# A tiled gated block with local attention on one core: its second row tile by feature halves, weights loaded in another order, orders anew

## The chip, the cores and the metric

The kernel runs on one core of a Trainium2 chip. The engines of a core work side by side and wait for one another by semaphores: TensorE (PE, matrix products; its weight loads are a row of their own, PEld), VectorE (DVE), ScalarE (ACT), GpSimd (POOL) and SyncE (SP), which here issues DMA transfers alone. ScalarE and GpSimd issue DMAs too. The metric is the device time of one execution in microseconds (us), as the median of several runs. The profile comes from one execution, which has a time of its own; the span is the part of it that the profile shows.

## The reference

All arrays are bfloat16. `x` has 2048 rows of 512 features.

```python
D, Df, H, Dh, W, dil = 512, 1792, 32, 16, 8, 2
xn = layernorm(x)                         # (x - mean) / sqrt(var + 1e-5), per row
q, k, v = split(xn @ wqkv)                # 32 heads of 16
# row s sees the rows s, s-2, ..., s-14 (those below 0 are masked)
logits[h, s, w] = sum_d q[h, s, d] * k[h, s - 2*w, d] * Dh ** -0.5
o[h, s] = sum_w softmax_w(logits)[h, s, w] * v[h, s - 2*w]
s = o @ wo
g = silu((gelu(xn @ w_gate) * (xn @ w_up)) @ w_down)
out = x + s * g
```

## The kernel before

*Tiles and stages.* The 2048 rows are 16 tiles of 128 (numbered 0 to 15) and 4 blocks of 512 (0 to 3); block 0 is tiles 0 to 3. The stages of a block are: layer norm; turning the normed rows, so that features lie on partitions (`xT`); q, k, v (`qkv_ps`); the scores of 8 keys per row (products on VectorE, `prod`; their sums over a head, block 0 by TensorE into `L_ps`, blocks 1 to 3 by 16 accumulating GpSimd DMAs each into `Ls`, the "gathers"); softmax; the products with v (`pv`) and their sums; a trip of the attention output through DRAM, which turns it; gate and up products (`g_ps`, `u_ps`), gelu, their product `hT`; the down product `y_ps`, silu; the output product `s_ps`, its gate, the sum with x and the store.

*What sets the order.* The program is not written in its order. Each step is an `Op` with an engine, an assumed duration, the steps that it needs (a leading `~` means only the start of the other), the buffers that it takes and frees, and a priority. `schedule` (L126) plays them through as a list scheduler: on each engine, of the steps that could start within 0.05 us of the earliest one, that with the lowest priority. The instructions are then written out in the order of those planned starts, and nothing reorders them afterwards: on each engine, and on each engine's DMA queue, they are issued in that order and each waits for its own semaphores. The assumed durations (`DMA_FIXED`, `DMA_RATE` and so on) thus decide orders and nothing else. A priority is a base per stage and block (`N`, `S`, `V`, `Q`, `F`, `Y`, `O` in `PARAMS`), plus an offset per step, plus a number of its own from the list `nudge` (one per step, 854 in all).

*The start.* Before the first data TensorE runs matmuls on zeros (`warm`, L254). `loads` (L1131) gives the order of the input transfers as one chain. Tile 0's x comes in two feature halves of 256, the first issued by SP, the second by ACT (L1135), tile 1's x whole by SP. Then the weights of q and of k, each in two halves of 256 KB by contraction chunks (L1146): both halves of q by ACT, both of k by SP; then x of tiles 2 and 3, the two halves of v's weights, x of block 1, and the ffn weights, all by SP.

*Block 0 by tiles.* Tile 0 is done by `first_tile` (statistics L463, root L466, reciprocal L471, norm L475, transposes L483, each by feature halves; the first half's copy into `xT0` by ACT, L490, the second's by VectorE, L492). Tiles 1 to 3 are done by `layernorm`: statistics of tile 1 in two halves of one loaded tile, one norm of 512 (L348), four transposes on TensorE (L365), one copy of 512 by ACT (L374) or, for the tiles in `vcopy` (tile 1), by VectorE (L372). `qkv_tiles` (L600) makes q, k and v of each tile, 16 matmuls of 128x128 each (L612). For q and k of tile 0 these are split in two steps of 8 (`mm_q0_t0a` and so on), the first of which needs only the first feature half of x and of the weights. TensorE's order at the start is: tile 0's transposes; q and the first half of k of tile 0; tile 1's four transposes; k's second half; q and k of tile 1; v of tile 0; v of tile 1; tile 2's work. The x of blocks 1 to 3 is turned by DMA (L440).

*Later names.* Products with the keys L705 and their halving sums L717, L721; gathers L798; the maximum over keys L810; products with v L868 and sums L875; stores and load of the turned output L1018 and L1027; gate and up products L925, gelu L941, evacuation of up L949, their product L963; down L985, silu L1001; output product L1046.

Of the kernel before, what the change touches and what calls it, by code (L numbers as in the profile page):

```python
# [44 lines left out]
DMA_FIXED = 2.3  # L45
DMA_CROWDED = 3.5
LOADED = 40.0
DMA_RATE = {"SP": 325e3, "POOL": 180e3}
# [11 lines left out]
    sums=(3,), warm=4, slack=2.82, N=[306.5, 111.8, 418.2, 728.4], psum=(0,), rpow=False,  # L60
    S=[237.0, -554.0, 60.7, -257.2], V=[-277.9, -35.1, 276.7, -102.3], Q=[43.7, -338.2, 71.3, 36.8],
    F=[34.7, 79.8, 266.5, 442.4], Y=[-106.0, 20.0, -72.7, -105.7], O=[19.3, -380.8, -324.0, 455.3], vnorm=(),
    vcopy=(1,), vsum=(0,), crowd=1.35,
    nudge=[
# [44 lines left out]
    ],  # L109
)  # L110


# [115 lines left out]
class Kernel:  # L228
# [53 lines left out]
    def layernorm(self, j):  # L282
        base = self.when("N", j)
        for tt in range(TPB):
# [12 lines left out]
            def half_stats(i):  # L297
                h = D // 2
                self.nc.vector.bn_stats(out=self.stats1[:, i, :], in_=self.x_sb[:, 1, i * h : (i + 1) * h])  # L299
# [76 lines left out]
            if t == 0:  # L376
                self.first_tile()
                continue
# [924 lines left out]
```

## Time and profile before

| | |
|---|---|
| median of 3 runs | 213.8 us (213.67, 213.80, 214.13) |
| the profiled execution's own time | 213.45 us |
| its span | 211.6 us, 3097 instructions |
| TensorE / VectorE / ScalarE / GpSimd busy | 98% / 88% / 74% / 31% of the span |
| granted TensorE clock | 1.0 |
| DMA | 32.17 MB in 32991 packets, mean 152 GB/s |

A page gives, for one execution, the busy time of each engine; the span in 40 slices; the DMA queues; the chain of work that ended last, followed back from the last instruction; the costliest groups of instructions, with the busy time, the mean duration of one in ns, and the idle time of the engine just before them with what ended most of it; and the DMA issues with the time from issue to landing. Views of the trace give the same by line, by wait, by stretch of time, and in order of time. An engine that is busy for 98% of the span can only be finished sooner by the other 2%, or by doing less.

### The profile page before, as it was taken

How to read it: one execution, taken by the hardware profiler on the slowest of the kernel's cores; microseconds unless marked ns; L12 is line 12 of the kernel's file. 1: busy time of each engine (PE TensorE's matmuls, PEld its weight loads, DVE VectorE, ACT ScalarE, POOL GpSimd, SP SyncE). 2: the span in 40 equal slices, each digit the busy share in tenths (PEclk: the TensorE clock that was granted, in tenths of full speed). 3: DMA queues.
4: the chain of work that ended last, by engine and by line, in shares of the span. 5: the costliest groups of instructions: out<-in, count | busy, mean ns of one | idle time of the engine just before them, and what ended most of it. 6: DMA issues, size and time to landing. Idle time of an engine off the chain costs nothing.

```text
span 211.6 us, 3097 instructions
## 1 busy us (share of the span) xinstructions
PE 206.6 (98%) x1123; PEld 101.4 (48%) x1123; DVE 187.3 (88%) x215; ACT 156.5 (74%) x262; POOL 65.7 (31%) x108
## 2 busy tenths in 40 slices
PE   7999999999999999999999999999999999999994
PEld 2996444445444444444445444444444444444442
DVE  4698998499999997999999999999999989998124
ACT  3688999999999998679634888967323689666352
POOL 5041310002137688040369422379630011001000
PEclk9999999999999999999999999999999999999999
DMA  6999997200938587680797947378996059505822
GB/s 191 364 382 373 318 288 184 58 0 22 176 100 159 102 159 147 142 206 7 112 159 126 167 137 169 74 114 161 153 180 150 0 124 222 153 0 112 217 72 99
DMA packets 32991, 32.17 MB, mean 152 GB/s; under 512 B 17088, under 2 KB 29520, under 8 KB 32976
## 3 DMA queue, kind: packets, MB, share of 16 engines
q0 software_dynamic: 5136, 14.41, 36.3%
q1 hardware_dynamic: 27008, 16.95, 29.2%
q10 hardware_dynamic: 832, 0.62, 0.9%
q8 instruction: 9, 0.15, 0.3%
q14 instruction: 6, 0.05, 0.1%
HBM read 14.12 MB, written 6.31 MB: 97 GB/s over the span
## 4 chain that ended last, share of the span: by engine, by line
PE 94%; DVE 2%; DMA 1%; ACT 1%; issue 0%; SPq 0%
PE g_ps L925 23%; PE u_ps L925 23%; PE y_ps L985 22%; PE qkv_ps L528 15%; PE s_ps L1046 6%; PE qkv_ps L612 5%; DMA x_sb<-in_A_x_dram 1%; DVE s L1101 1%; DVE s L1107 0%; ACT s L1061 0%; ACT xnT L374 0%; PE L_ps L742 0%; PE tr_ps L365 0%; DVE xnT L372 0%; DVE stats L299 0%
## 5 line engine op out<-in xcount | busy, mean ns | idle before, releaser
L925 PE MATMUL g_ps<-xnT,wg_sb 128*128 128x512 bf16 x224 | 54.2, 380 | 0.0
L925 PE MATMUL u_ps<-xnT,wu_sb 128*128 128x512 bf16 x224 | 53.6, 379 | 0.0
L985 PE MATMUL y_ps<-wd_sb,hT 128*128 128x512 bf16 (+2 forms) x238 | 51.8, 367 | 0.0
L798 POOL DMA_DIRECT2D Ls<-prod x48 | 36.9, 872 | 27.2 <-DMA Ls<-prod 12.4
L941 ACT ACTIVATE gl<-g_ps 128x512 bf16<-128x512 f32 x56 | 31.9, 598 | 16.0 <-PE g_ps L925 12.8
L705 DVE TENSOR_TENSOR prod<-q_sb,k_sb 128x2048 bf16<-128x2048 bf16 x32 | 37.8, 1219 | 2.2 <-ACT q_sb L543 1.7
L949 ACT ACTIVATE hT<-u_ps 128x512 bf16<-128x512 f32 x56 | 32.1, 601 | 7.9 <-PE u_ps L925 6.8
L868 DVE TENSOR_TENSOR pv<-attn,v_arr 128x4096 bf16<-128x4096 bf16 x16 | 36.2, 2284 | 0.1
L985 PEld LDWEIGHTS <-hT 128*128 128x128 bf16 x238 | 22.7, 98 | 25.9
L925 PEld LDWEIGHTS <-wu_sb 128*128 128x128 bf16 x224 | 21.9, 98 | 26.4
L925 PEld LDWEIGHTS <-wg_sb 128*128 128x128 bf16 x224 | 21.7, 98 | 26.1 <-issue 0.4
L963 DVE TENSOR_TENSOR hT<-hT,gl 128x1024 bf16<-128x1024 bf16 x28 | 18.6, 683 | 3.0 <-ACT gl L941 2.6
L570 POOL DMA_DIRECT2D vT_dram<-vst x12 | 8.9, 745 | 35.5 <-ACT vst L550 35.4
L717 DVE TENSOR_TENSOR prod<-prod 128x2048 bf16<-128x2048 bf16 x16 | 19.2, 1220 | 0.0
L1061 ACT ACTIVATE s<-s_ps 128x512 bf16<-128x512 f32 x15 | 8.8, 597 | 12.6 <-PE s_ps L1046 12.6
L677 POOL DMA_DIRECT2D v_arr<-vT_dram x16 | 10.8, 719 | 16.3 <-DMA vT_dram<-vst 16.3
L1046 PE MATMUL s_ps<-wo_sb,oT_sb 128*128 128x512 bf16 (+2 forms) x68 | 15.6, 367 | 0.0
L875 DVE TENSOR_TENSOR pv<-pv 128x2048 bf16<-128x2048 bf16 x12 | 14.5, 1220 | 0.1
L941 ACT ACT_TABLE_LOAD x10 | 12.8, 1283 | 0.7 <-PE g_ps L925 0.6
L1001 ACT ACTIVATE sil<-y_ps 128x512 bf16<-128x512 f32 (+2 forms) x17 | 9.3, 574 | 5.3 <-PE y_ps L985 5.2
L1074 POOL DMA_DIRECT2D s<-x_sb x3 | 2.8, 930 | 31.3 <-DVE tot L835 15.7
L528 PE MATMUL qkv_ps<-xnT,wq_sb 128*128 128x512 bf16 x48 | 12.0, 379 | 0.0
(94 smaller groups left out, 230.3 us busy)
## 6 DMA issues: line engine op xcount, KB each, us to landing
Ls<-prod POOLq DMA_DIRECT2D x48, 128.0 KB, 3.5
v_arr<-vT_dram POOLq DMA_DIRECT2D x16, 142.0 KB, 4.4
vT_dram<-vst POOLq DMA_DIRECT2D x16, 128.0 KB, 3.7
pv<-pv POOLq DMA_DIRECT2D x4, 512.0 KB, 4.9
oT_dram<-o_sb SPq DMA_DIRECT2D x16, 128.0 KB, 3.4
oT_sb<-oT_dram SPq DMA_DIRECT2D x4, 512.0 KB, 4.7
wg_sb<-in_B_w_gate_dram SPq DMA_DIRECT2D x2, 896.0 KB, 9.9
wu_sb<-in_B_w_up_dram SPq DMA_DIRECT2D x2, 896.0 KB, 12.3
```

The source lines that it names most:

```text
L528: self.nc.tensor.matmul(ps[:], lhsT=self.w_qkv(which, dk, c), rhs=self.t[f"xT{j}"][:, dk, :], start=(dk == 0), stop=(dk == NC - 1),)
L705: self.nc.vector.tensor_tensor(out=self.t[pair][:, c % 2].rearrange("p n w t -> p w n t"), in0=q.unsqueeze(1).to_broadcast([P, W, 2, P]), ...
L717: self.nc.vector.tensor_tensor(out=pr[:, 0], in0=pr[:, 0], in1=pr[:, 1], op=ALU.add)
L798: self.nc.gpsimd.dma_start(out=self.t[f"Ls{j}"][H * tq : H * (tq + 1)], in_=self.t[f"pr{j}_{tq // 2}_0"][s::NC, 0, tq % 2], **(dict(accum_ ...
L868: self.nc.vector.tensor_tensor(out=pv[:], in0=self.t[f"at{j}"][:, 2 * i : 2 * i + 2, :].unsqueeze(2).to_broadcast([P, 2, DH, P]), in1=win, ...
L875: self.nc.vector.tensor_tensor(out=pv[:, 0], in0=pv[:, 0], in1=pv[:, 1], op=ALU.add)
L925: nc.tensor.matmul(ps[:], lhsT=w[:, dk, fc * P : (fc + 1) * P], rhs=self.t[f"xT{j}"][:, dk, :], start=(dk == 0), stop=(dk == NC - 1),)
L941: self.nc.scalar.activation(out=self.t[f"gl{j}_{pair}"][:, fc % 2, :], in_=self.t[f"ps_g{j}_{fc}"][:], func=AF.Gelu_apprx_tanh,)
L949: self.nc.scalar.activation(out=self.t[f"h{j}"][:, fc, :], in_=self.t[f"ps_u{j}_{fc}"][:], func=AF.Copy)
L963: self.nc.vector.tensor_tensor(out=h, in0=h, in1=self.t[f"gl{j}_{pair}"][:], op=ALU.mult)
L985: nc.tensor.matmul(self.t["ps_" + key][:, 0 : n1 - n0], lhsT=self.t[f"h{j}"][:, fc, tt * P : (tt + 1) * P], rhs=self.wd_sb[:, fc, n0:n1], ...
L1046: self.nc.tensor.matmul(ps[:, 0 : n1 - n0], lhsT=self.t[f"oT{j}"][:, c, tt * P : (tt + 1) * P], rhs=self.wo_sb[:, c, n0:n1], start=(c == 0 ...
```

## The change

- Tile 1 goes through the same function as tile 0, now `early_tile(t)`: its x is loaded in two halves (the first by SP, the second by ACT), with two statistics, two norms of 256, two pairs of transposes into buffers of their own and two copies of 256, both by VectorE. Its q is split in two steps of 8 matmuls, as tile 0's.
- Weights of q, k, v: the first halves of q and k are issued by ACT, the second halves by SP; v comes as one transfer of 512 KB.
- Tile 2's copy of 512 goes from ACT to VectorE (`vcopy`).
- Tile 3's statistics are not put before tile 2's.
- Two branches of code that did not run (`power`, `minus`) are removed, and a memset for one of them on GpSimd.
- The planner's assumed DMA durations, the bases of the priorities and the whole list `nudge` (now 858 numbers) are replaced.

The built program has the same 1123 matmuls. Its order on TensorE at the start: q of tile 0, first half of k, tile 1's transposes, second half of k, first half of q of tile 1, k of tile 1, v of tile 0, second half of q of tile 1, tile 2's transposes, v of tiles 1 and 2, then tile 3. On ACT's queue: second halves of x of tiles 0 and 1, first halves of q's and k's weights (the instruction for k's also waits for the landing of tile 0's half, whose DMA slot it uses again). On SP's: first halves of x of tiles 0 and 1, second halves of q's and k's weights, x of tiles 2 and 3, v's weights, x of block 1 and on as before. Later many steps stand elsewhere in their engine's order; the order of the last ones is the old one.

```diff
-DMA_FIXED = 2.3
-DMA_CROWDED = 3.5
+DMA_FIXED = 2.0
+DMA_CROWDED = 3.8
+SHARED = 1.14
 LOADED = 40.0
-DMA_RATE = {"SP": 325e3, "POOL": 180e3}
+DMA_RATE = {"SP": 370e3, "POOL": 180e3}
...
 PARAMS = dict(
-    sums=(3,), warm=4, slack=2.82, N=[306.5, 111.8, 418.2, 728.4], psum=(0,), rpow=False,
-    S=[237.0, -554.0, 60.7, -257.2], V=[-277.9, -35.1, 276.7, -102.3], Q=[43.7, -338.2, 71.3, 36.8],
-    F=[34.7, 79.8, 266.5, 442.4], Y=[-106.0, 20.0, -72.7, -105.7], O=[19.3, -380.8, -324.0, 455.3], vnorm=(),
-    vcopy=(1,), vsum=(0,), crowd=1.35,
+    sums=(3,), psum=(0,), warm=4, slack=2.52, N=[340.7, 50.8, 416.1, 741.4], S=[213.7, -605.4, 61.2, -265.3],
+    V=[-291.2, -67.1, 282.9, -169.4], Q=[-35.5, -339.1, 71.0, 39.1], F=[17.7, 79.3, 268.5, 442.6],
+    Y=[-110.3, 20.9, -73.3, -165.5], O=[19.3, -378.8, -317.6, 380.6], vnorm=(), vcopy=(2,), vsum=(0,),
+    crowd=1.35,
     nudge=[
...
-            if t == 0:
-                self.first_tile()
+            if t < 2:
+                self.early_tile(t)
                 continue
...
-            elif t == 1:
-                self.op("stats1_0", "DVE", 0.34, ["ld_x1_0", "~aggr0"], lambda f=half_stats: f(0), prio=prio)
-                self.op("stats1_1", "DVE", 0.34, ["ld_x1_0", "~norm0_1"], lambda f=half_stats: f(1), prio=prio)
-                self.op("aggr1", "DVE", 0.16, ["stats1_0", "stats1_1"], half_aggr, prio=prio)
             else:
                 self.op(f"stats{t}", "DVE", 0.61,
-                        [f"ld_x{t if j == 0 else j}_{j}"] + (["copy1"] if t == 2 else []), stats, prio=prio,
+                        [f"ld_x{t if j == 0 else j}_{j}"] + {2: ["copy1"], 3: ["~aggr2"]}.get(t, []), stats, prio=prio,
...
-    def first_tile(self):
+    def early_tile(self, t):
 
         h = D // 2
         xn = {}
 
         def stats(i):
-            self.nc.vector.bn_stats(out=self.stats0[:, i, :], in_=self.x_sb[:, 0, i * h : (i + 1) * h])
+            self.nc.vector.bn_stats(out=self.stats2[:, t, i, :], in_=self.x_sb[:, t, i * h : (i + 1) * h])
 
         def aggr():
-            self.nc.vector.bn_aggr(out=self.mv[:, 0, :], in_=self.stats0[:])
+            self.nc.vector.bn_aggr(out=self.mv[:, t, :], in_=self.stats2[:, t])
 
         def root():
             self.nc.scalar.activation(
-                out=self.rstd[:, 0, :], in_=self.mv[:, 0, 1:2], func=AF.Sqrt, bias=self.eps[:]
+                out=self.rstd[:, t, :], in_=self.mv[:, t, 1:2], func=AF.Sqrt, bias=self.eps[:]
             )
 
         def inverse():
-            self.nc.vector.reciprocal(out=self.rstd[:, 0, :], in_=self.rstd[:, 0, :])
+            self.nc.vector.reciprocal(out=self.rstd[:, t, :], in_=self.rstd[:, t, :])
 
         def norm(i):
-            xn[i] = self.new(f"xn0_{i}", [P, h], BF16, "xn")
+            xn[i] = self.new(f"xn{t}_{i}", [P, h], BF16, "xn")
             self.nc.vector.tensor_scalar(
-                out=xn[i][:], in0=self.x_sb[:, 0, i * h : (i + 1) * h], scalar1=self.mv[:, 0, 0:1],
-                scalar2=self.rstd[:, 0, :], op0=ALU.subtract, op1=ALU.mult,
+                out=xn[i][:], in0=self.x_sb[:, t, i * h : (i + 1) * h], scalar1=self.mv[:, t, 0:1],
+                scalar2=self.rstd[:, t, :], op0=ALU.subtract, op1=ALU.mult,
             )
 
         def turn(i):
-            ps = self.new(f"tr0_{i}", [P, 2, P], BF16, "tr_ps")
+            ps = self.new(f"tr{t}_{i}", [P, 2, P], BF16, "tr_ps")
             for c in range(2):
                 self.nc.tensor.transpose(ps[:, c, :], xn[i][:, c * P : (c + 1) * P], self.ident[:])
 
         def copy(i):
-            if i == 0:
+            if t == i == 0:
                 self.new("xT0", [P, NC, TQ], BF16, "xnT")
-            out = self.t["xT0"][:, 2 * i : 2 * i + 2, 0:P]
-            if i == 0:
+            out = self.t["xT0"][:, 2 * i : 2 * i + 2, t * P : (t + 1) * P]
+            if t == i == 0:
                 self.nc.scalar.activation(out=out, in_=self.t["tr0_0"][:], func=AF.Copy)
             else:
-                self.nc.vector.tensor_copy(out=out, in_=self.t["tr0_1"][:])
-
-        prio = -60.0
+                self.nc.vector.tensor_copy(out=out, in_=self.t[f"tr{t}_{i}"][:])
+
+        prio = -60.0 + 10 * t
+        order = {(1, 0): ["~aggr0"], (1, 1): ["~norm0_1"]}
         for i in range(2):
-            self.op(f"stats0_{i}", "DVE", 0.34, [f"ld_x0_0{'ab'[i]}"], lambda i=i: stats(i), prio=prio)
-        self.op("aggr0", "DVE", 0.1, ["stats0_0", "stats0_1"], aggr, prio=prio)
-        self.op("root0", "ACT", 0.25, ["aggr0"], root, prio=prio, table="sqrt")
-        self.op("rstd0", "DVE", 0.07, ["root0"], inverse, prio=prio)
+            self.op(f"stats{t}_{i}", "DVE", 0.34, [f"ld_x{t}_0{'ab'[i]}"] + order.get((t, i), []), lambda i=i: stats(i),
+                    prio=prio)
+        self.op(f"aggr{t}", "DVE", 0.16, [f"stats{t}_0", f"stats{t}_1"], aggr, prio=prio)
+        self.op(f"root{t}", "ACT", 0.27, [f"aggr{t}"], root, prio=prio, table="sqrt")
+        self.op(f"rstd{t}", "DVE", 0.1, [f"root{t}"], inverse, prio=prio)
         for i in range(2):
-            self.op(f"norm0_{i}", "DVE", 0.26, ["rstd0"] + ["~norm0_0"] * i, lambda i=i: norm(i), take=[("xn", f"xn0_{i}")],
-                    use=[f"xn0_{i}"], prio=prio + i)
-            self.op(f"turn0_{i}", "PE", 2 * MM128, [f"norm0_{i}"] + ["~turn0_0"] * i, lambda i=i: turn(i),
-                    take=[("F", f"tr0_{i}")], use=[f"xn0_{i}", f"tr0_{i}"], prio=prio)
-        self.op("copy0_0", "ACT", 0.28, ["turn0_0"], lambda: copy(0), take=[("xT", "xT0")],
-                use=["tr0_0", "xT0"], prio=prio)
-        self.op("copy0", "DVE", 0.22, ["turn0_1", "~copy0_0"], lambda: copy(1), use=["tr0_1", "xT0"], prio=prio)
+            self.op(f"norm{t}_{i}", "DVE", 0.26, [f"rstd{t}"] + [f"~norm{t}_0"] * i, lambda i=i: norm(i),
+                    take=[("xn", f"xn{t}_{i}")], use=[f"xn{t}_{i}"], prio=prio + i)
+            self.op(f"turn{t}_{i}", "PE", 2 * MM128, [f"norm{t}_{i}"] + [f"~turn{t}_0"] * i, lambda i=i: turn(i),
+                    take=[("F", f"tr{t}_{i}")], use=[f"xn{t}_{i}", f"tr{t}_{i}"], prio=prio)
+            name = f"copy{t}" + "_0" * (1 - i)
+            need = [f"turn{t}_{i}"] + ([f"~copy{t}_0"] if i else ["copy0"] if t else [])
+            self.op(name, "DVE" if t or i else "ACT", 0.24 if t or i else 0.3, need, lambda i=i: copy(i),
+                    take=[] if t or i else [("xT", "xT0")], use=[f"tr{t}_{i}", "xT0"], prio=prio)
...
-                if t == 0 and which < 2:
+                if (t, which) in ((0, 0), (0, 1), (1, 0)):
                     half = NC * NC // 2 * MM128
-                    self.op(f"mm_{key}a", "PE", half, ["copy0_0", weights + "a"], lambda f=mms: f(0, 2), take=take,
+                    self.op(f"mm_{key}a", "PE", half, [f"copy{t}_0", weights + "a"], lambda f=mms: f(0, 2), take=take,
                             use=use, prio=prio)
-                    self.op(f"mm_{key}", "PE", half, [f"mm_{key}a", "copy0", weights], lambda f=mms: f(2, NC),
+                    self.op(f"mm_{key}", "PE", half, [f"mm_{key}a", f"copy{t}", weights], lambda f=mms: f(2, NC),
...
-        x0 = [("ld_x0_0a", lambda: x_tile(0, 0, D // 2), kb),
-              ("ld_x0_0b", lambda: x_tile(0, D // 2, D, "scalar"), kb),
-              xt[1]]
+        early = [(f"ld_x{t}_0{'ab'[i]}", lambda t=t, i=i: x_tile(t, i * D // 2, (i + 1) * D // 2, ("sync", "scalar")[i]),
+                  64 * kb if t or i else kb) for t in range(2) for i in range(2)]
         h = NC // 2
-        wq = [("ld_wqa", lambda: w_qkv(0, 0, h, "scalar"), 256 * kb), ("ld_wq", lambda: w_qkv(0, h, NC, "scalar"), 256 * kb)]
-        wk = [("ld_wka", lambda: w_qkv(1, 0, h), 256 * kb), ("ld_wk", lambda: w_qkv(1, h, NC), 256 * kb)]
-        wv = [("ld_wva", lambda: w_qkv(2, 0, h), 256 * kb), ("ld_wv", lambda: w_qkv(2, h, NC), 256 * kb)]
+        wq = [("ld_wqa", lambda: w_qkv(0, 0, h, "scalar"), 256 * kb), ("ld_wq", lambda: w_qkv(0, h, NC), 256 * kb)]
+        wk = [("ld_wka", lambda: w_qkv(1, 0, h, "scalar"), 256 * kb), ("ld_wk", lambda: w_qkv(1, h, NC), 256 * kb)]
+        wv = [("ld_wv", lambda: w_qkv(2), 512 * kb)]
         xb = [(f"ld_x{j}_{j}", lambda j=j: x_block(j), 512 * kb) for j in range(NJ)]
-        seq = x0 + wq + wk + [xt[2], xt[3]] + wv + [xb[1]]
+        seq = early + wq + wk + [xt[2], xt[3]] + wv + [xb[1]]
...
-                    nbytes=int(nbytes * (self.par["crowd"] if i >= len(seq) - 5 else 1)))
+                    nbytes=int(nbytes * (1.0 if i < 12 else SHARED if i < len(seq) - 5 else SHARED * self.par["crowd"])))
```

More of the change, by code (lines that the diff above doesn't have):

```diff
@@ L295, in aggr @@
                 nc.vector.bn_aggr(out=self.mv[:, t, :], in_=self.stats[:, t, :])
-            def half_stats(i):
-                h = D // 2
-                self.nc.vector.bn_stats(out=self.stats1[:, i, :], in_=self.x_sb[:, 1, i * h : (i + 1) * h])
-            def half_aggr():
-                self.nc.vector.bn_aggr(out=self.mv[:, 1, :], in_=self.stats1[:])
             def root(t=t):
@@ L330, in product @@
                 )
-            def power(a, b, k):
-                nc = self.nc
-                r = self.rstd[:, a:b, 0]
-                nc.gpsimd.tensor_scalar(
-                    out=r, in0=self.mv[:, a:b, 1], scalar1=k, scalar2=EPS, op0=ALU.mult, op1=ALU.add
-                )
-                nc.gpsimd.tensor_tensor(out=r, in0=r, in1=self.mhalf[:, 0 : b - a], op=ALU.pow)
-                nc.gpsimd.tensor_tensor(out=self.nmr[:, a:b, 0], in0=self.mv[:, a:b, 0], in1=r, op=ALU.mult)
-            def minus(a, b):
-                m = self.mv[:, a:b, 0]
-                self.nc.vector.tensor_scalar(out=m, in0=m, scalar1=-1.0, scalar2=None, op0=ALU.mult)
             def norm_dve(t=t):
@@ L412, in layernorm @@
                 a, b = j * TPB, (j + 1) * TPB
-                if tt == 0 and self.par["rpow"]:
-                    need = [f"aggr{i}" for i in range(a, b)]
-                    if not by_act:
-                        self.op(f"minus{j}_", "DVE", 0.1, need, lambda f=minus, a=a, b=b: f(a, b), prio=prio)
-                        need = [f"minus{j}_"]
-                    self.op(f"shift{j}_", "POOL", 2.0, need,
-                            lambda f=power, a=a, b=b, k=1.0 / D if by_act else 1.0: f(a, b, k), prio=prio, slack=0.5)
-                elif tt == 0:
+                if tt == 0:
                     self.op(f"root{j}_", "ACT", 0.25, [f"aggr{i}" for i in range(a, b)],
@@ L430, in layernorm @@
                 self.op(f"norm{t}", "ACT", 0.75, [ready], norm_act, take=[("xn", f"xn{t}")],
-                        use=[f"xn{t}"], prio=prio, slack=(3.0 if self.par["rpow"] else 0.5) if j else 0.0)
+                        use=[f"xn{t}"], prio=prio, slack=0.5 if j else 0.0)
             else:
@@ L807, in gathered @@
                 before = [nm]
+        hot = -10.0
         def peak():
@@ L818, in less @@
             )
-        hot = -10.0
         self.op(f"peak{j}", "DVE", 1.9, [f"gat{j}_{tq}_{NC - 1}" for tq in range(TPB)], peak, use=[f"Ls{j}"], prio=hot)
@@ L1228 @@
     k.stats = cpool.tile([P, NT, nc.vector.BN_STATS_DIM], F32, name="stats")
-    k.stats1 = cpool.tile([P, 2, nc.vector.BN_STATS_DIM], F32, name="stats1")
-    k.stats0 = cpool.tile([P, 2, nc.vector.BN_STATS_DIM], F32, name="stats0")
+    k.stats2 = cpool.tile([P, 2, 2, nc.vector.BN_STATS_DIM], F32, name="stats2")
     k.mv = cpool.tile([P, NT, nc.vector.BN_AGGR_DIM], F32, name="mv")
     k.rstd = cpool.tile([P, NT, 1], F32, name="rstd")
-    k.mhalf = cpool.tile([P, TPB], F32, name="mhalf")
     k.eps = cpool.tile([P, 1], F32, name="eps")
@@ L1241 @@
     k.rs = cpool.tile([P, 2, P], BF16, name="rs")
+    k.ind = cpool.tile([P, H], BF16, name="ind")
     k.ident = cpool.tile([P, P], BF16, name="ident")
-    k.ind = cpool.tile([P, H], BF16, name="ind")
     k.mask = cpool.tile([H, W, PAD], F32, name="mask")
@@ L1252 @@
     make_identity(nc, k.ident[:])
-    nc.gpsimd.memset(k.mhalf[:], -0.5)
     nc.gpsimd.memset(k.ind[:], 1.0)
```

88 rows, old and new, of the table nudge are left out of this document.

## The prediction

> **What bounds the kernel now.** I read the page first (busy shares, chain), then the waits of PE, the chain in order of time, the busy time by stretch, and last the timeline and the landings of the loads.
>
> ```profile
> span 211.6 us, 3097 instructions
> ...
> PE 206.6 (98%) x1123; PEld 101.4 (48%) x1123; DVE 187.3 (88%) x215; ACT 156.5 (74%) x262; POOL 65.7 (31%) x108
> ...
> PE 94%; DVE 2%; DMA 1%; ACT 1%; issue 0%; SPq 0%
> ```
>
> The chain is PE for 94% of the span. An engine share can hide waits, so the next view is what PE waited for, then its busy time by stretch (each row: length, then PE, PEld, DVE, ACT, POOL, with counts, clock, DMA).
>
> ```profile
> PE warm_ps L254 <- DVE eps L1251: 1.3, 1, 1.3
> PE tr_ps L483 <- DVE xn L475: 0.2, 1, 0.2
> PE qkv_ps L612 <- ACT xnT L490: 0.2, 1, 0.2
> ```
> ```profile
> 20.00:35.00 15.00, 15.00 (x70) 6.64 (x68) 14.83 (x22) 14.37 (x25) 3.34 (x5) 1.00 1.04 289
> 125.00:150.00 25.00, 25.00 (x118) 11.30 (x117) 24.72 (x25) 20.02 (x34) 15.02 (x22) 1.00 0.65 130
> 150.00:175.00 25.00, 25.00 (x117) 11.30 (x116) 24.11 (x23) 11.93 (x19) 3.94 (x5) 1.00 0.58 118
> ```
>
> From 20 us on PE has no gap, at granted clock 1.00. No reordering can gain there; it can only lose. What is left to win lies in the start, so that is read in order of time:
>
> ```profile
> 5.07 0.30 PE tr_ps L483 x2
> ...
> 5.39 0.39 ACT xnT L490
> 5.78 0.04 issue
> 5.82 1.50 PE qkv_ps L612 x24
> ...
> 7.58 0.43 DVE xnT L372
> ...
> 8.06 2.85 PE qkv_ps L612 x48
> ...
> 11.43 0.60 ACT xnT L374
> ...
> 12.07 1.05 PE qkv_ps L612 x16
> ```
>
> The chain leaves PE three times after its first transposes: for tile 0's copy (5.39), tile 1's copy (7.58) and tile 2's copy (11.43). The timeline prices the last two (a group's length includes the last matmul's tail, so starts are compared):
>
> ```profile
> 3.94 0.29 ACT L466 ACTIVATE rstd<-mv,eps 128x1 f32<-128x1 f32 x1 [0.70 <-DVE mv L463]
> 4.13 0.43 DVE L299 BATCH_NORM_STATS2 stats<-x_sb 128x6 f32<-128x256 bf16 x1 [0.23 <-DMA x_sb<-in_A_x_dram]
> 4.48 0.15 DVE L471 RECIPROCAL rstd<-rstd 128x1 f32<-128x1 f32 x1
> 7.16 0.39 PE L365 MATMUL tr_ps<-ident,xn 128*128 128x128 bf16 x4
> 7.38 0.61 PE L612 MATMUL qkv_ps<-xnT,wk_sb 128*128 128x128 bf16 x8
> 8.95 1.06 PE L612 MATMUL qkv_ps<-xnT,wk_sb 128*128 128x128 bf16 x16
> 9.84 1.05 PE L612 MATMUL qkv_ps<-xnT,wv_sb 128*128 128x128 bf16 x16
> 10.96 1.06 PE L612 MATMUL qkv_ps<-xnT,wv_sb 128*128 128x128 bf16 x16
> ```
>
> 16 of these matmuls take 9.84 − 8.95 = 0.89 us, one 0.0556; four transposes 7.38 − 7.16 = 0.22. The eight of k's second half end at 7.38 + 0.45 = 7.83, and q of tile 1 starts at 8.06: 0.23 us lost to tile 1's copy. The sixteen of v end at 10.96 + 0.89 = 11.85 and the next starts at 12.07: 0.22 lost to tile 2's copy.
>
> **The change part by part.**
>
> *x of tile 1 in halves on both queues.* VectorE stood 0.23 us for x1; its first statistics then ran into the time at which tile 0's reciprocal could have started (ACT's root was done at 3.94 + 0.29 = 4.23, the reciprocal came at 4.48). The halves go out right behind tile 0's, each ahead of all weights of its queue. If they land by 3.9, those statistics (0.43) start right before ACT's root and the reciprocal at about 4.28; everything of tile 0 moves up 0.20 and q's first matmul from 5.82 to 5.62. If they land as before, at 4.1, this is nothing. I take 0.20; the next term shows that it does not decide.
>
> *The weights' order.* Rows of q, k and v (issues, first and last start; landings after issue):
>
> ```profile
> L1146 ACTq DMA_DIRECT2D wq_sb<-in_A_wqkv_dram x2: 427/442/457, 1.2 to 1.8; - x2
> DMA to landing us min/median/max: 3.3/3.8/4.3
> ...
> L1146 SPq DMA_DIRECT2D wk_sb<-in_A_wqkv_dram x2: 435/452/469, 1.7 to 2.2; - x2
> DMA to landing us min/median/max: 4.2/4.4/4.6
> ...
> L1146 SPq DMA_DIRECT2D wv_sb<-in_A_wqkv_dram x2: 379/406/433, 3.7 to 4.5; - x2
> DMA to landing us min/median/max: 4.6/4.6/4.7
> ```
>
> So q's halves landed at 4.5 and 6.1, k's at 5.9 and 6.8, v's last at 9.1. Afterwards the first halves of q and k go out by ACT, the second halves by SP, so both halves of one matrix travel side by side. q's first half, issued at about 1.8 instead of 1.2 (ACT issues x1's half in its old place), should land between the old 4.5 and 6.1; I take the middle, 5.3, which is free, since it is needed at 5.62 (6.1 would cost 0.5). k's first half is the new risk: ACT's instruction for it also waits for tile 0's first x (a DMA slot that is used again), and it now shares the engines with k's second half. Bounds: 5.9, its old landing, and 6.8, where the second half, the last of the same 1,280 KB (x of two tiles, q, k), landed. I take 6.7, nearer to the later, because two equal halves end together. PE could start k at 5.62 + 16 × 0.0556 = 6.51; with 6.7 and the 0.04 that an issue costs it starts at 6.74, a new wait of 0.23, with tile 1's transposes behind it in PE's order.
>
> *Tile 1 by feature halves.* Behind k's first eight (to 7.19) and the transposes (to 7.41) stand k's second eight (to 7.85). VectorE's rows by shape:
>
> ```profile
> L348 DVE TENSOR_SCALAR xn<-x_sb,mv,rstd 128x512 bf16<-128x512 bf16 x2 | 0.8, 416 | 0.1
> L475 DVE TENSOR_SCALAR xn<-x_sb,mv,rstd 128x256 bf16<-128x256 bf16 x2 | 0.6, 343 | 0.0
> L372 DVE COPY xnT<-tr_ps 128x512 bf16<-128x512 bf16 x1 | 0.4, 424 | 0.8 <-PE tr_ps L365 0.8
> L492 DVE COPY xnT<-tr_ps 128x256 bf16<-128x256 bf16 x1 | 0.2, 237 | 0.0
> ```
>
> The first half's copy waits for two transposes (tail of 0.22 included, to about 7.5) and takes 0.24 in place of 0.42: done near 7.75, before PE is free at 7.85. So q's first half of tile 1 starts at 7.85 in place of 8.06: **0.21 us gained**, the 0.20 and the 0.23 of the old gap less the new wait. VectorE pays 2 × 0.343 − 0.416 + 2 × 0.237 − 0.424 = 0.32 us, beside the 0.8 us in which it stood waiting for the transposes.
>
> PE's new order is then q half (8), k (16), v of tile 0 (16), q's other half. v starts at 7.85 + 24 × 0.0556 = 9.19, and v's weights, now one transfer behind the same 2,048 KB, should land at 9.1 as before: just in time. This also caps the part: were k early, v would wait. If v lands at 9.4, 0.2 us is given back; if at 8.9, the gain may grow by 0.2.
>
> *Tile 2's copy by VectorE* (0.42 for 0.60 on ACT): v of tile 1, 0.89 us, now stands between tile 2's transposes and their first user; tail 0.22 + copy 0.42 + two hand-overs of 0.04 make 0.72. **0.22 us gained**, and nothing if VectorE is not free then. Its 0.42 us lie in the start too, where its order puts them ahead of the first product (1.22 us).
>
> *The orders anew.* PE has the same 1,123 matmuls and the end keeps its order, so from 13 us on this is worth 0 at best.
>
> Sum: 0.21 + 0.22 = 0.43. The profiled execution took 213.45 us (span 211.6 and 1.85 around it): 213.02, span 211.17. The median of the runs shown is 213.8, 0.35 above it, so the forecast is 213.37, 0.2% faster. About 0.2%, 0.43 us, is what a measurement of this kernel can tell from no change, and the forecast stands on that edge.
>
> **The rivals.**
>
> *The start gets no shorter: k's halves come late.* The Trainium skill ("DMA: Bandwidth & Descriptors", section "Issuing engines are not separate DMA queues") says that DMAs started from different engines run on the same 16 engines and interleave, so that spreading them saves the issue only. The trace agrees: q's second half by ACT and k's first by SP, issued at 1.8 and 1.7, landed together, at 6.1 and 5.9. By that mechanism k's two halves land together at 6.8, k starts at 6.88 and the gain is 0.29: 213.5. With a gap of 0.3 between x1 and the weights, which nothing here excludes, it is 7.1, and the gain is about 0: 213.8. Against it: x1 stands ahead of the weights with half the bytes on each queue. Chance 0.22.
>
> *A later stall, slower.* The place is VectorE at block 3's scores, near 158 us. Rows of before: the gathers, the product that follows, the reduction that reads them, and VectorE's last wait before the end.
>
> ```profile
> L798 POOL DMA_DIRECT2D Ls<-prod x48: 513/812/1762, 64.1 to 154.6; - x48
> ...
> DMA to landing us min/median/max: 2.7/3.5/7.4
> ...
> 159.33 2.29 DVE L868 TENSOR_TENSOR pv<-attn,v_arr 128x4096 bf16<-128x4096 bf16 x1
> ...
> 162.67 1.91 DVE L810 TENSOR_REDUCE peak<-Ls 128x128 f32<-128x1024 f32 x1
> ...
> 196.99 0.69 DVE L963 TENSOR_TENSOR hT<-hT,gl 128x1024 bf16<-128x1024 bf16 x1 [2.12 <-ACT gl L941]
> ```
>
> The last of the 48 gathers was issued at 154.6 and landed by 158.1, over 4 us before the reduction. In the new order two sums that stood ahead of the reduction stand behind it, and block 1's output is summed two products sooner, so its stores run beside these gathers. A gather at the worst latency in place of the median is 3.9 us late; 2.1 us of that fits into VectorE's wait at 197, and 1.8 reach PE's last products: 215.2. It decides from about 2 us of delay. For it: VectorE has 0.3 and 0.9 us idle in the two quoted stretches. Against it: PE has ready work of other blocks all along. Chance 0.24.
>
> *The loads land sooner* (v by 8.9, k by 6.5): 213.2, chance 0.08. The forecast's case has the remaining 0.46.
>
> **How the numbers follow.** Faster by over 0.2%: most of the forecast's case (its landings may fall either way, 0.34 of 0.46) and the sooner loads, 0.42. Within 0.2%: the rest of it and late k, 0.34. Slower: 0.24. The likeliest case alone is 213.1 to 213.7. The range takes in early loads below and most later stalls above: 213.0 to 214.8, with a tenth left out above it.
>
> **What would show it.** Right: PE's first L612 matmul near 5.6, a gap of about 0.2 before k's weights (released by their DMA), none before tile 1's q or after tile 2's transposes, v starting at 9.2, and no PE gap after 13 us but the short one at the tiled sums. Wrong: k's weights after 7.0, a PE wait on VectorE or ACT after 100 us, or a VectorE wait on the gathers of over 2 us.

## The result, and the profile after

The changed kernel takes 214.67 us (median of 20 runs, 214.12 to 216.69), the kernel before in as many runs 213.80: a ratio of 1.0059, 95% interval 1.0040 to 1.0079. It is slower by 0.6%. The profiled execution took 215.84 us, with a span of 214.0, 2.4 above the 211.6 of before. The page of after (span, busy shares, chain):

```profile
span 214.0 us, 3081 instructions
...
PE 206.7 (97%) x1105; PEld 102.7 (48%) x1123; DVE 187.8 (88%) x218; ACT 149.1 (70%) x256; POOL 65.6 (31%) x107
...
PE 94%; DMA 4%; issue 1%; DVE 0%; ACT 0%
```

TensorE's work is the same (1123 weight loads; 18 matmuls have no record in this trace), but DMA has gone from 1% to 4% of the chain. The chain of after, in order of time (start, length, what):

```profile
0.81 2.11 DMA x_sb<-in_A_x_dram
2.92 0.02 issue
2.95 5.47 DMA wk_sb<-in_A_wqkv_dram
8.42 0.05 issue
8.46 1.04 PE qkv_ps L585 x8
```

These five rows are the main part of the answer: tile 0's x lands at 2.92; its DMA slot (the semaphore that tells of its landing, the same one for both transfers in the trace) is then used again for the first half of k's weights, issued at 2.95; that lands at 8.42, and k's first matmul starts at 8.46. Before, k started 16 matmuls after q's 5.82, at 6.71. TensorE before, at these places and at tile 2's transposes:

```profile
5.82 1.05 PE L612 MATMUL qkv_ps<-xnT,wq_sb 128*128 128x128 bf16 x16 [0.21 <-ACT xnT L490]
6.71 0.61 PE L612 MATMUL qkv_ps<-xnT,wk_sb 128*128 128x128 bf16 x8
...
10.74 0.39 PE L365 MATMUL tr_ps<-ident,xn 128*128 128x128 bf16 x4
```

The timeline of TensorE after adds q and the speed of the matmuls:

```profile
6.75 1.33 PE L585 MATMUL qkv_ps<-xnT,wq_sb 128*128 128x128 bf16 x16 [1.30 <-DMA wq_sb<-in_A_wqkv_dram]
8.46 1.04 PE L585 MATMUL qkv_ps<-xnT,wk_sb 128*128 128x128 bf16 x8 [0.39 <-DMA wk_sb<-in_A_wqkv_dram]
9.30 0.63 PE L453 MATMUL tr_ps<-ident,xn 128*128 128x128 bf16 x4
9.72 1.06 PE L585 MATMUL qkv_ps<-xnT,wk_sb 128*128 128x128 bf16 x8
...
13.39 0.39 PE L346 MATMUL tr_ps<-ident,xn 128*128 128x128 bf16 x4
```

q waits 1.30 us for its weights (6.75 in place of 5.82), k another 0.39 behind q. And from 8.46 to 9.30 eight matmuls take 0.84 us, 0.105 each, where the kernel before took 0.0556: TensorE runs at half rate. The stretches of after show it in the granted clock (third number from the right; behind each stretch stand its length and the busy time of PE, PEld, DVE, ACT and POOL), and show the rest of the kernel unharmed:

```profile
5.00:7.40 2.40, 1.10 (x16) 0.79 (x16) 1.57 (x7) 0.68 (x2) 0.00 (x0) 1.00 1.08 370
7.40:10.80 3.40, 3.01 (x31) 2.75 (x29) 1.04 (x3) 0.60 (x1) 0.00 (x0) 0.51 1.10 359
10.80:14.20 3.40, 3.40 (x63) 3.40 (x62) 2.12 (x10) 2.61 (x7) 0.15 (x1) 0.99 1.06 379
...
110.00:160.00 50.00, 49.74 (x229) 23.15 (x232) 49.90 (x44) 30.80 (x51) 28.27 (x38) 1.00 0.77 143
```

The half rate lasts from 7.4 to 10.8. Not every execution has it, as the run again shows below; this one is the fifth longest of the 20. Late in the kernel TensorE has no wait (the 0.26 us that are missing in 50 are records that the trace lacks); no wait of it after 9 us is in the list of waits.

**One mark for all runs.** In every version the same matmuls stand ahead of tile 2's four transposes. In the kernel before these start at 10.74, with the 0.22 us for tile 2's copy still to come: 10.96. If nothing behind that point matters, each span must be 211.6 + (start of tile 2's transposes − 10.96). It is so in all profiles, to 0.1 us:

| run | k's first matmul | tile 2's transposes | span so worked out | span measured | median us (runs) | ratio to before, 95% |
|---|---|---|---|---|---|---|
| before | 6.71 | 10.74 + 0.22 | | 211.6 | 213.80 (20) | |
| changed | 8.46 | 13.39 | 214.0 | 214.0 | 214.67 (20) | 1.0040 to 1.0079 |
| again | 8.48 | 13.25 | 213.9 | 213.9 | 215.57 (7) | 1.0046 to 1.0100 |
| oldloads | 6.64 | 10.91 | 211.6 | 211.5 | 213.52 (11) | 0.9953 to 0.9995 |
| x1_by_sp | 6.90 | 11.09 | 211.7 | 211.7 | 213.65 (12) | 0.9977 to 0.9997 |
| w_as_before | 9.07 | 14.31 | 215.0 | 214.9 | 216.95 (4) | 1.0130 to 1.0164 |
| filler | 8.66 | 12.49 | 213.1 | 213.1 | 214.80 (12) | 1.0017 to 1.0054 |
| k_by_sp | 7.36 | 11.15 | 211.8 | 211.8 | 213.92 (12) | 0.9982 to 1.0033 |
| x1_behind | 8.50 | 13.78 | 214.4 | 214.4 | 214.38 (12) | 1.0000 to 1.0053 |
| weights_first | 7.99 | 11.80 | 212.4 | 212.4 | 214.47 (12) | 0.9998 to 1.0062 |
| x1_whole | 6.93 | 10.72 | 211.4 | 211.4 | 213.39 (12) | 0.9965 to 1.0002 |
| x1_whole_v | 6.98 | 10.88 | 211.5 | 211.6 | 213.45 (12) | 0.9960 to 1.0006 |
| b_weights | 7.28 | 11.30 + 0.22 | 212.2 | 212.2 | 213.99 (12) | 0.9990 to 1.0020 |
| copy2_act | 7.03 | 10.82 + 0.26 | 211.7 | 211.7 | 213.63 (12) | 0.9980 to 0.9999 |

(The span is that of one execution, the median that of all; the profiled executions of the changed kernel, again, w_as_before and x1_behind had the half rate behind k's first matmul. A ratio is to the runs of the kernel before on the same chip, with a median of 213.97, for the changed kernel 213.80, for copy2_act 213.81.) So in the profiled executions the new later orders cost and bring nothing, and what stands ahead of tile 2's transposes decides everything.

### The profile page after: what moved, and what is told of

Read it like the earlier page. It is cut to its first block, busy times and chain, and to the rows that moved or that the text cites. A ratio compares the mean times of both kernels' runs of the same rounds, so it can differ in the third digit from the quotient of the medians.

```text
span 214.0 us, 3081 instructions
## 1 busy us (share of the span) xinstructions
PE 206.7 (97%) x1105; PEld 102.7 (48%) x1123; DVE 187.8 (88%) x218; ACT 149.1 (70%) x256; POOL 65.6 (31%) x107
## 4 chain that ended last, share of the span: by engine, by line
PE 94%; DMA 4%; issue 1%; DVE 0%; ACT 0%
PE u_ps L899 23%; PE y_ps L959 22%; PE g_ps L899 22%; PE qkv_ps L501 15%; PE s_ps L1020 6%; PE qkv_ps L585 5%; DMA wk_sb<-in_A_wqkv_dram 3%; DMA x_sb<-in_A_x_dram 1%; PE L_ps L715 0%; PE tr_ps L346 0%; PE tr_ps L453 0%; DVE s L1075 0%; ACT sil L975 0%; DVE s L1081 0%
## 5 line engine op out<-in xcount | busy, mean ns | idle before, releaser
L771 POOL DMA_DIRECT2D Ls<-prod x48 | 37.4, 871 | 24.2 <-issue 11.0
L915 ACT ACTIVATE gl<-g_ps 128x512 bf16<-128x512 f32 x56 | 31.9, 599 | 15.8 <-PE g_ps L899 10.8
L865 POOL DMA_DIRECT2D pv<-pv x4 | 3.8, 958 | 35.1 <-DVE pv L842 35.1
L501 PE MATMUL qkv_ps<-xnT,wv_sb 128*128 128x512 bf16 x47 | 11.9, 379 | 0.1
```

What stands on the lines that cost most here:

```text
L501: self.nc.tensor.matmul(ps[:], lhsT=self.w_qkv(which, dk, c), rhs=self.t[f"xT{j}"][:, dk, :], start=(dk == 0), stop=(dk == NC - 1),)
L771: self.nc.gpsimd.dma_start(out=self.t[f"Ls{j}"][H * tq : H * (tq + 1)], in_=self.t[f"pr{j}_{tq // 2}_0"][s::NC, 0, tq % 2], **(dict(accum_ ...
L915: self.nc.scalar.activation(out=self.t[f"gl{j}_{pair}"][:, fc % 2, :], in_=self.t[f"ps_g{j}_{fc}"][:], func=AF.Gelu_apprx_tanh,)
```

## The experiments

All are the changed kernel with a small edit, mostly of its loads, but for b_weights, which edits the kernel before. The edits are written short. Except where it is said, the order of instructions on TensorE, VectorE and GpSimd stays that of the changed kernel.

**again: the changed kernel once more.**

> The changed kernel once more. Theory (loads): in the profile of it TensorE waited 1.30 us for q's first weights and 0.39 for k's, and its clock then fell to half for about 3 us. The granted clock of 1.00 in most of its 20 runs says that the fall is not always there, so a run without it should show the same late landings (q's first half 6.0 to 6.7, k's first half 7.5 to 8.4), TensorE's first q matmul at 6.2 to 6.7, a span of 212.4 to 213.0 and a time of 214.3 to 214.7. Rival (the later orders lose it): first q matmul by 5.8 in such a run, and the loss in gaps after 13 us.

Measured: 215.57 us (214.02 to 216.36). The landings are late again. TensorE's timeline in this run:

```profile
6.29 1.90 PE L585 MATMUL qkv_ps<-xnT,wq_sb 128*128 128x128 bf16 x16 [0.79 <-DMA wq_sb<-in_A_wqkv_dram]
8.48 1.04 PE L585 MATMUL qkv_ps<-xnT,wk_sb 128*128 128x128 bf16 x8 [0.30 <-DMA wk_sb<-in_A_wqkv_dram]
9.32 0.63 PE L453 MATMUL tr_ps<-ident,xn 128*128 128x128 bf16 x4
...
10.57 0.61 PE L585 MATMUL qkv_ps<-xnT,wq_sb 128*128 128x128 bf16 x8
```

The expectation held for the landings (k's at its late edge) and missed the time and the span (213.9 in place of 212.4 to 213.0), for a reason that the clock column hides: it says 1.00 over the whole start, but 8 matmuls from 8.48 to 9.32 again take 0.105 us each. Here TensorE never reached its full rate before 10.5. So the granted clock in these records doesn't show a rate that was low from the start on; the distance from start to start does. The 27 runs of the changed kernel spread from 214.0 to 216.7, 11 of them over 215.2. Seven of these 11 show a mean granted clock of 0.99, the 16 others 0.998 or more; of the four high ones at 1.00 this one alone is profiled, and whether the other three are like it is not shown.

**oldloads, x1_by_sp, w_as_before: which load is it?** Two edits, in three runs (oldloads has both; x1_by_sp the first; w_as_before the second):

```diff
-x_tile(t, ..., ("sync", "scalar")[i])
+x_tile(t, ..., ("sync", "sync" if t else "scalar")[i])
...
-("ld_wq", lambda: w_qkv(0, h, NC), 256 * kb)
+("ld_wq", lambda: w_qkv(0, h, NC, "scalar"), 256 * kb)
-("ld_wka", lambda: w_qkv(1, 0, h, "scalar"), 256 * kb)
+("ld_wka", lambda: w_qkv(1, 0, h), 256 * kb)
```

> The changed kernel with all loads on the queues of before: x of tile 1 in its two halves, but both by SP; both halves of q's weights by ACT, both of k's by SP. Every engine's order is otherwise that of the changed kernel. Theory (loads): q's first half lands at 4.5 to 4.9 again, first q matmul at 5.6 to 5.8, and the two gaps that the change closes (0.21 and 0.22) come out: 213.2 to 213.6, no fall of the clock. Rival (the later orders lose it): 214.2 to 214.7, as the changed kernel.

> The changed kernel with the second half of tile 1's x issued by SP in place of ACT, and nothing else; q's and k's first halves stay on ACT, their second halves on SP. Rival A (x1's half ahead of q's weights on ACT's queue is what makes them late): q's first half is issued at 1.3 and lands by 5.0, and 213.3 to 213.8. Rival B (the halves of one matrix side by side are what makes them late): q's first half lands at 5.8 or later and the time is 214.1 or more.

> The changed kernel with both halves of q's weights by ACT and both of k's by SP, as before, and x of tile 1 on both queues, as changed. Rival B (halves side by side): q's first half lands by 5.3 and 213.3 to 213.8. Rival A (x1's half ahead of q's weights): q's first half still starts late and lands at 5.8 to 6.5; besides, q's second half stands on ACT where k's first half stood, behind the wait for a used DMA slot (issue at 2.9), and lands near 8: 214.5 to 216.

Measured: 213.52, 213.65 and 216.95 us. TensorE's rows of oldloads:

```profile
5.64 1.05 PE L585 MATMUL qkv_ps<-xnT,wq_sb 128*128 128x128 bf16 x16 [0.22 <-ACT xnT L460]
6.64 0.64 PE L585 MATMUL qkv_ps<-xnT,wk_sb 128*128 128x128 bf16 x8
...
7.54 0.64 PE L585 MATMUL qkv_ps<-xnT,wk_sb 128*128 128x128 bf16 x8
8.02 0.61 PE L585 MATMUL qkv_ps<-xnT,wq_sb 128*128 128x128 bf16 x8
...
9.56 1.07 PE L585 MATMUL qkv_ps<-xnT,wv_sb 128*128 128x128 bf16 x16
```

With the loads put back, everything else of the change works: q starts at 5.64, 0.18 sooner than before, and q of tile 1 follows k's second half without a gap (7.54 + 8 × 0.0556 = 7.98, next start 8.02). The loss is in the loads. x1_by_sp then says in which: moving the second half of tile 1's x from ACT's queue to SP's, with the new weights' order kept, undoes the loss, to within 0.13 us of oldloads. Rival A holds, rival B falls. w_as_before is its mirror: ACT's queue holds x's half, then both halves of q; the second half of q stands behind the slot wait, and the chain shows

```profile
2.89 5.48 DMA wq_sb<-in_A_wqkv_dram
8.37 0.05 issue
8.42 1.61 PE qkv_ps L585 x15
```

Its 216.95 us are above the 216 that rival A allowed; the profiled execution also ran at half rate behind this wait (k's first eight from 9.07 to 9.92), which the expectation had not counted.

**k_by_sp and x1_behind: x's half on ACT does two things; which one costs?** It puts q's first half 0.5 us later (issued at 1.8 in place of 1.3), and it makes k's first half the transfer that meets a used slot (2.95 in place of 1.8). Each run undoes one of the two (for x1_behind the planned slots stay, and transfers change places in them):

```diff
# k_by_sp
-("ld_wka", lambda: w_qkv(1, 0, h, "scalar"), 256 * kb)
+("ld_wka", lambda: w_qkv(1, 0, h), 256 * kb)
# x1_behind: order of issue
-x0a, x0b, x1a, x1b, wqa, wqb, wka, wkb
+x0a, x0b, x1a, wqa, wqb, x1b, wka, wkb
```

> The changed kernel with the first half of k's weights issued by SP, ahead of the second, in place of ACT, where it waits for a used DMA slot; q's first half stays behind x on ACT. Theory A1 (k's first half behind the slot wait is the larger part): it is issued at 2.2, lands by 7.1, k follows q without a wait, 213.8 to 214.5. Theory A2 (q's first half, still issued at 1.8, is the larger part): q starts at 6.2 or later with the clock at half, and 214.8 or more.

> The changed kernel with two issues on ACT exchanged: q's first half ahead of the second half of tile 1's x. k's first half stays on ACT behind the slot wait. Theory A1 (the slot wait is the larger part): q starts at 5.6 to 5.8, but k's first half is still issued at 2.9 and lands at 7.8 to 8.4, so that TensorE waits 1.0 to 1.6 us for it: 214.4 to 215.2. Theory A2 (q's late first half is the larger part): 213.4 to 214.0.

Measured: 213.92 and 214.38 us. First k_by_sp, then x1_behind, on TensorE:

```profile
6.03 1.50 PE L585 MATMUL qkv_ps<-xnT,wq_sb 128*128 128x128 bf16 x16 [0.52 <-DMA wq_sb<-in_A_wqkv_dram]
7.36 0.61 PE L585 MATMUL qkv_ps<-xnT,wk_sb 128*128 128x128 bf16 x8
```
```profile
5.74 1.21 PE L585 MATMUL qkv_ps<-xnT,wq_sb 128*128 128x128 bf16 x16 [0.21 <-ACT xnT L460]
8.50 1.04 PE L585 MATMUL qkv_ps<-xnT,wk_sb 128*128 128x128 bf16 x8 [1.55 <-DMA wk_sb<-in_A_wqkv_dram]
```

k_by_sp came out as theory A1 has it; x1_behind at the lower edge of A1 (214.38 where 214.4 was its lowest), above A2's 214.0. In k_by_sp k starts 0.65 us later than before. Only 0.21 of it is q's late start (6.03 for 5.82). The other 0.44 is the rate again: q's 16 matmuls take 7.36 − 6.03 = 1.33 us in place of 0.89, with the first nine starts 0.107 us apart in the trace, under a granted clock of 1.00. The closed gaps (0.23 and 0.22) pay most of it back: no change against before. With q on time, k is still 1.79 late. The slot wait is the larger part.

**filler: what does the half rate cost?**

```diff
 self.new("ps_" + key, [P, NC, P], F32, "qkv_ps")
+for _ in range({"q0_t0": 5, "k0_t0": 4}.get(key, 0) if a == 0 else 0):
+    matmul(ps, lhsT=blank[:, 0:P], rhs=blank, start=True, stop=True)
```

> The changed kernel with nine matmuls on zeros added on TensorE, into the buffers that the next product overwrites: five between tile 0's transposes and q, four between q and k. They do no useful work (9 x 0.216 = 1.9 us at full clock) and lie in the two waits for weights, if the landings stay as they are. Theory (the waits themselves cost less than the fall of TensorE's clock that they bring): with no idle stretch the clock stays, 128-column matmuls take 0.056 us from q on, and the time falls to 214.2 to 214.8 although work was added, below the repeated changed kernel's 215.6. Rival (the clock's fall has nothing to do with the idle stretch, or is small): 215.6 or more.

Measured: 214.80 us, and every run within 214.25 to 215.16. Its rows on TensorE (L584 are the fillers; its other lines stand 4 lower):

```profile
5.30 1.74 PE L584 MATMUL qkv_ps<-blank 128*128 128x512 bf16 x5
6.88 1.06 PE L589 MATMUL qkv_ps<-xnT,wq_sb 128*128 128x128 bf16 x16
7.77 1.03 PE L584 MATMUL qkv_ps<-blank 128*128 128x512 bf16 x4
8.66 0.64 PE L589 MATMUL qkv_ps<-xnT,wk_sb 128*128 128x128 bf16 x8
9.14 0.39 PE L453 MATMUL tr_ps<-ident,xn 128*128 128x128 bf16 x4
```

Nine matmuls of no use were added, k starts later still (8.66), and yet tile 2's transposes come at 12.49 in place of 13.39 and 13.25, for k's eight now take 9.14 − 8.66 = 0.48. So the idle stretch brings the half rate, worth about 1 us where it falls on these matmuls. The filler doesn't make the version good; it takes the high times away (none of 12 over 215.2, where the changed kernel had 11 of 27). What it leaves, a span of 213.1, is the late landing without the half rate.

**x1_whole, x1_whole_v, weights_first: versions meant to beat both.** Old loads, but x of tile 1 as one transfer; the same with v ahead of tile 3's x; and one with q's and k's weights ahead of the second half of x.

In all three q's weights go by ACT and k's by SP, as in oldloads.

```diff
# x1_whole: order of issue
-x0a, x0b, x1a, x1b, wqa, wqb, wka, wkb, x2, x3, wv
+x0a, x0b, x1, wqa, wqb, wka, wkb, x2, x3, wv
# x1_whole_v
+x0a, x0b, x1, wqa, wqb, wka, wkb, x2, wv, x3
# weights_first
+x0a, x0b, x1a, wqa, wka, wqb, x1b, wkb, x2, wv, x3
```

> The changed kernel with all its loads as before the change: x of tile 1 as one transfer by SP, both halves of q's weights by ACT, both of k's by SP (v stays one transfer). Tile 1 is still worked by feature halves, tile 2 copied by VectorE. Theory: one issue less on SP puts k's halves back to 5.9 to 6.2 and 6.8 to 7.1 and v to 9.1 to 9.3, so that the 0.1, 0.2 and 0.2 us for which TensorE still waited with the old loads and two halves of x mostly go, though q starts at 5.8 again: 213.1 to 213.5. Rival (tile 1's x as one transfer holds up its statistics and with them tile 0's reciprocal): 213.6 to 213.9.

> The same with v's weights ahead of x of tile 3 on SP's queue. Theory: v lands 0.3 earlier, at 8.8 to 9.0, before TensorE wants it, so this gains only what was left of the wait for v: 0 to 0.2 us below the run without it, 213.0 to 213.4. Rival (x of tile 3, later by some 1.4 us, holds up tile 3): 213.6 or more.

> A version meant to beat both: the changed kernel with q's weights by ACT right behind x of tile 0 (both halves), k's first half by SP ahead of the second half of tile 1's x, and v's weights ahead of x of tile 3. In the run with the old loads TensorE still waited 0.1, 0.2 and 0.2 us for k's first and second half and for v. Theory: k's first half lands by 6.2, k's second by 7.0, v by 9.1, and some 0.2 to 0.4 us of those waits go: 213.1 to 213.4 where the run with the old loads took 213.5. Rival (tile 1's x, now later, holds its transposes up): 213.5 to 213.9.

Measured: 213.39, 213.45 and 214.47 us. x1_whole is the lowest median of all, 0.58 below the 213.97 that the kernel before took beside it (ratio 0.9983), but its interval of 0.9965 to 1.0002 takes in 1; those of oldloads (0.45 below), x1_by_sp and copy2_act end just below 1. x1_whole_v adds nothing, 0.05 past what was expected: the wait for v was already gone, since in x1_whole v follows k of tile 1 at once. weights_first is a miss, and lies above its rival's 213.9 too; the cause is tile 1's late x, as the rival says, but through another tile. VectorE in it:

```profile
6.66 0.43 DVE L430 BATCH_NORM_STATS2 stats<-x_sb 128x6 f32<-128x256 bf16 x1 [1.55 <-DMA x_sb<-in_A_x_dram]
7.12 0.21 DVE L433 BATCH_NORM_AGGREGATE mv<-stats 128x2 f32<-128x12 f32 x1
7.25 0.24 DVE L462 COPY xnT<-tr_ps 128x256 bf16<-128x256 bf16 x1
```

VectorE works in order: the statistics of tile 1's second half wait for x until 6.66, and behind them stands tile 0's second copy (7.25), for which q's second half waits on TensorE. A load that seemed to have time held up another tile.

**b_weights and copy2_act: the two parts that were left.** The weights' queues of the changed kernel in the kernel before; and x1_whole with tile 2's copy back on ACT.

```diff
# b_weights
-wq: ACT, ACT; wk: SP, SP
+wq: ACT, SP; wk: ACT, SP
# copy2_act
-if t in self.par["vcopy"]:
+if t == -1:
     self.nc.vector.tensor_copy(...)
```

> The kernel before with the weights' queues of the changed one and nothing else: first halves of q's and k's weights by ACT, second halves by SP, x of tile 1 whole by SP as before. Theory (it is x of tile 1 on ACT's queue that costs, not the weights' order): q's first half lands at 4.5 to 4.8, k's first half at 5.6 to 6.0, q's second half at 5.9 to 6.4, and the time is within 0.3 us of the kernel before. Rival (two halves of one matrix side by side come later): q's second half after 6.6 and a loss of 0.4 us or more.

> The version with x of tile 1 whole, and tile 2's copy back on ACT at the same place of the order. Theory (VectorE's copy closes the old gap): ACT finishes tile 0's v and tile 1's q first, its copy of 0.60 us starts at 11.2 to 11.5 and ends at 11.8 to 12.1, while the sixteen matmuls of tile 1's v end at 11.8: TensorE waits 0 to 0.25 us for it, and the time is 213.4 to 213.7. Rival (tile 1's v between the transposes and their user is what closes the gap, on either engine): no wait, and 213.4 or less, since VectorE is free for its products 0.4 us sooner.

Measured: 213.99 us, the kernel before beside it 213.97; and 213.63, before beside it 213.81. The weights' order in the kernel before makes no difference that can be told (0.9990 to 1.0020), although q's second half landed at 6.76, as the rival has it, and k's first matmul in the profiled execution came at 7.28 in place of 6.71; the rival's loss of 0.4 us is not in the medians. For copy2_act, TensorE's matmuls and ACT's copy among them, then the same matmuls of x1_whole:

```profile
11.05 2.21 PE L585 MATMUL qkv_ps<-xnT,wv_sb 128*128 128x128 bf16 x32
...
11.55 0.60 ACT L355 ACTIVATE xnT<-tr_ps 128x512 bf16<-128x512 bf16 x1
```
```profile
10.95 1.95 PE L585 MATMUL qkv_ps<-xnT,wv_sb 128*128 128x128 bf16 x32
```

The 32 matmuls of v take 2.21 us in place of 1.95: a wait of 0.26 in their middle. The theory holds: the gap closes only with VectorE's copy, and the new order on TensorE alone leaves it.

## Why the prediction was wrong

- **The landing of k's first half (the sum's step "I take 6.7, nearer to the later") failed, and it is what turned the sign.** It landed at 8.42. The prediction named the wait for a used DMA slot and then bounded the landing by 5.9 and 6.8, rows of transfers issued at 1.7 and 2.2. But that wait has a time: it ends with tile 0's x, at 2.92, and 2.9 plus the 4.2 to 4.6 that the quoted k rows show from issue to landing is 7.1 to 7.5, outside both bounds. The rows to see most of the loss were there; the wait was named and not put into the sum. The remaining 0.9 to 1.3 us is the time from issue to landing, 5.47 here and 5.43 in x1_behind; no run takes it apart.
- **The landing of q's first half (5.3, bounds 4.5 and 6.1) was too early:** TensorE waited for it until 6.75, 6.29 (again) and 6.03 (k_by_sp), two of them past the later bound. The middle was taken though the transfer had lost its head start. Busy time by stretch from 3 to 4 us, before and after:

```profile
3.00:4.00 1.00, 1.00 (x4) 0.39 (x3) 0.86 (x3) 0.29 (x3) 0.94 (x10) 1.00 0.98 318
```
```profile
3.00:4.00 1.00, 1.00 (x4) 0.39 (x3) 0.96 (x4) 0.24 (x3) 0.94 (x10) 1.00 0.67 51
```

  Before, with q's first half issued at 1.2, 318 GB/s moved in this stretch. After, no weight was issued before 1.7, and only 51 GB/s moved: 0.27 MB, about one half of a matrix, is missing there. The other runs agree: 253 GB/s or more where q's first half was issued at 1.2 to 1.3, at most 101 where it was issued at 1.8.
- **The half rate of TensorE was in no step and in no rival.** k's 1.75 us less the closed 0.23 would put tile 2's transposes at 10.74 + 1.75 − 0.23 = 12.26; they came at 13.39. The remaining 1.1 us is the half rate. The same sum gives 12.46 for filler (measured 12.49) and 11.16 for k_by_sp (11.15), which ran at full rate from k on. So of the 2.4 us by which the profiled span grew, 1.3 is the landing and 1.1 the rate. The median lost 0.87: it lies among the executions up to 215.2, whose spans of 212.3 to 213.3 are near the 212.9 that the landing alone gives. By the Trainium skill ("TensorE: Matmul & The Clock Gate", section "What's actually happening") the clock depends on how busy TensorE was in a window of 3413 ns that runs freely. The trace agrees in the length: 7.4 to 10.8.
- **The two gains were right in kind; their sum is shown only by the medians.** Tile 1's copy no longer holds q up (oldloads, 8.02) and tile 2's gap of 0.22 is gone, which copy2_act brings back as 0.26. The 0.20 at q's first matmul was 0.18 in oldloads. With the old loads the medians are 0.45 to 0.58 below the kernel before, for the 0.43 that was forecast. The profiled executions show less: tile 2's transposes come 0.05 (oldloads) and 0.24 us (x1_whole) before the old mark of 10.96. Waits for weights take part back in oldloads (k's second half starts 0.2 us behind the transposes, v 0.2 us behind k, a landing that the prediction priced so), and the profiled execution of the kernel before was a quick one, 213.45 for a median of 213.80.
- **The rivals.** Late k weights had the right mechanism and too small a price: 213.5 to 213.8, by a landing of 6.8 to 7.1. The later stall at block 3, the only case that ended slower, didn't come: TensorE has no wait after 9 us, and the later orders are worth 0, as the forecast said. That 214.67 lies inside the range of 213.0 to 214.8 is luck: its upper part stood for this stall.
- **Of the signs named,** "k's weights after 7.0" was the one that came.

What stays open: why so little moves before 4 us when the first weights are issued at 1.7 to 1.8, and why only some executions are caught at half rate; both were seen, neither was taken apart.

## What to carry to other kernels

A DMA instruction that has to wait for a used slot has an issue time: look up when the transfer that it waits for lands, add the latency of the nearest row, and put that into the sum. At the start of a kernel, ask of every transfer that is put ahead of another what it takes from the one behind it: 64 KB of x ahead of the first weights on ACT's queue cost more than the two gaps of 0.2 us that the change closed. And a short wait of TensorE early on can cost twice, once as a wait and once as a slower rate behind it, so price both.

## What the runs showed of the hardware

- TensorE fell to half rate (0.105 us per 128-column matmul for 0.056) after a wait of 1.30 us, for 3.4 us. The Trainium skill ("TensorE: Matmul & The Clock Gate", section "HAM oscillation — how this bites in real kernels") warns of idle gaps above some 3.4 us; here the fall came with a far shorter one: in the 2.4 us ahead of it TensorE was busy for 1.10. With matmuls on zeros in the waits (filler) it did not come.
- In one execution (again) the rate was at half from the first matmul on until 10.5 us, and the granted clock in the profile's rows says 1.00 throughout. In k_by_sp the same holds for the first nine matmuls of q. The start-to-start distance of like matmuls is the safer reading.
- Over the changed kernel's 27 runs the times spread over 2.7 us, over filler's 12 runs, with TensorE kept busy, over 0.9.
